# Four places of their own for the last full slot's row tiles, scaled by ScalarE, in a fused attention and mixture-of-experts kernel

## The chip, the cores and the metric

The kernel runs on one core of one Trainium2 chip. The metric is device time in microseconds (us); lower is better. The engines are named as the profile names them: PE is TensorE (PEld its weight loads), DVE is VectorE, ACT is ScalarE, POOL is GpSimd, SP is SyncE, which here only issues DMAs. L499 is line 499 of the kernel before.

## What is computed

A sigmoid attention gives 3584 tokens of 768 numbers; a gate sends each token to one of eight experts, which is two matrix products with a relu between them, and the row that comes out is scaled by two gate values.

```python
# q, k, v: (8, 12, 448, 64); x: N = 3584 tokens of D = 768; E = 8 experts, F = 1024
scores = scale * np.matmul(q, k.transpose(0, 1, 3, 2)) - np.log(S)
x = np.matmul(1.0 / (1.0 + np.exp(-scores)), v)      # then (B, H, S, D) -> (B*S, H*D)
e_idx = np.argmax(x @ w_gate, axis=1)
for e in range(E):
    mask = e_idx == e
    h = np.maximum(x[mask] @ w1[e], 0.0)
    ye = h @ w2[e]
    out[mask] = gate_w[mask, None] * eom[mask, e, None] * ye
```

## The kernel before

**Stages.** The first part of the program is the attention; it writes the rows of x to `x_dram` and, batch by batch, puts each token into the list of its expert. The second part works through *slots*: one slot is up to 448 tokens (`TB`, a full slot) or up to 240 tokens (`TM`, a partial slot) of one expert. How many slots of each kind there are is known only at run time; with this input nine run, seven full ones and then two partial ones. The last four full slots and the two partial ones stand behind branches on two counts, `full` and `part`. Where the count of full slots is used up, the program leaves that chain (the "exit") and goes to the partial slots, `half(0)`, `half(1)` and so on, each again behind a test of `part`.

**One slot.** `slot` (L542) runs layer 1 in eight steps f (L550): 18 matmuls each, three for every one of the six pieces of the depth, because each operand is split into a rounded part and a rest (`split`, L408: ACT casts, DVE subtracts). After each step ACT takes the product out of PSUM with a relu (L471) and DVE forms its rest (L472). Three PSUM places serve these products in turn (`psh`), so PE can't begin a fourth before ACT has emptied the first. In steps 1 to 4 `split_w2` splits the slot's own second weights, and behind them SP loads the first weights of the next slot (`load_w1`), which lie in the same bytes of the tile `plain` (`w1r`, `w2r`). POOL gathers the next slot's rows by an indirect DMA (L384), one or two per step. Then DVE turns these rows (`turn_x`, L429), and layer 2 follows, beside which the next slot's first weights and rows are split (`split_w1`, `split_x`, both L409 on ACT and L410 on DVE) and its second weights are loaded (`load_w2`, L395). A load into the bytes of `w1r` can only go once DVE has subtracted the weights that stood there.

**The two kinds of layer 2.** A full slot computes it in six groups of output columns (`layer2_columns`); DVE turns each back into `yq`. The sixth group is left in PSUM for the next slot, in `self.left`. A partial slot computes two row tiles t in two halves n each (`layer2`, L488): ACT scales a half into the place y (L499), and after n = 1 POOL scatters the 128 rows to `out` by an indirect DMA (L502, L537).

**What is left over.** `finish` (L504) is a generator that brings a full slot's 448 rows to `out`, in pieces between the next slot's work. Its first piece turns back the sixth group and has SP store `yq` to `y_dram` in eight DMAs (L515). The second loads two of the four row tiles back, 128 rows each and the fourth 64, into two places `ys` (L521). The third scales these two by the token weights (L526 on POOL, or L528 on ACT), scatters them, and loads the other two tiles into the same two places, which must wait until the scatters have read them. The fourth scales and scatters these. After a full slot ACT scales; behind the exit, where the weights were copied to `left_w` and `lt` is None, POOL does.

**`half(0)` in the code.** It finishes the last full slot while it computes its own rows. Its `finish` gets the places `hb` and `ys[1]`. The piece that loads tiles 0 and 1 runs at step 6 of layer 1 (L564), the piece that scales them and loads tiles 2 and 3 runs ahead of layer 2 (L578), the last piece after the first half tile (i == 0, L590). Its own two row tiles both use `ys[0]` (L582), so ACT's first write for tile 1 waits until the scatter of tile 0 has read that place. `half(1)` has nothing left to finish and uses `ys[0]` and `ys[1]`.

**Order.** The order on each engine is the program's order (`manual_schedule`); waits between engines follow from the tiles' bytes. Two scatters to `out` are taken to touch the same bytes and so wait for each other, except those that `finish` declares free of each other (L531). In `constants` and `route_tiles` four arrays of the routing, `lg`, `oh`, `turn`, `num`, are tiles of their own.

Of the kernel before, what the change touches and what calls it, by code (L numbers as in the profile page):

```python
# [8 lines left out]
F32 = mybir.dt.float32  # L9
# [3 lines left out]
AF = mybir.ActivationFunctionType  # L13
ALU = mybir.AluOpType
# [8 lines left out]
DM = H * D  # L23
DF = 1024
NT = B * S
HS = S // 2
NB = HS // 32
NCH = -(-NB // 2)
Q4 = DM // 4
G = 2  # L30
TB = 448
TM = 240
GB_, GM = TB // 32, -(-TM // 32)
# [14 lines left out]
XG = GB_ * Q4 * 4  # L48
# [3 lines left out]
def r32(ap):  # L52
    return ap.bitcast(F32)


class Kernel:
# [19 lines left out]
    def memory(self):  # L76
        self.rounded = self.pool("rounded").tile([128, ROUNDED // 4], F32R, name="rounded")
        self.plain = self.pool("plain").tile([128, PLAIN // 4], F32, name="plain")
        ps = self.pool("psum", space=PSUM).tile([128, 8, 512], F32, name="ps")
        self.ps_s = [ps[:, 0:2], ps[:, 2:4]]  # L80
        self.ps_o = [[ps[:, 4], ps[:, 5]], [ps[:, 6], ps[:, 7]]]
        self.ps_s2 = ps[:, 6:8]
        self.psh = [ps[:, i] for i in (0, 1, 2)]
        self.psy = [ps[:, i] for i in (4, 5, 3)]
        self.ps_step = [ps[:, i, 0:8] for i in (7, 3)]
        self.rot = {}
        self.beat = [None, None]
        self.hints = {2: [ET.Activation, ET.DVE, ET.Pool], 5: [ET.PE]}

        c = self.carve  # L90
        w = c(0, 3, 2, 2, DF)
        self.w1s = [[w[:, d // 2, a, d % 2] for d in range(6)] for a in range(2)]
        self.w1p = [[w[:, k, a] for k in range(3)] for a in range(2)]
        self.xs = [c(12 * DF * 4 + i * 6 * TB * 4, 6, TB) for i in range(2)]

        self.w1r = c(0, 6, DF, dt=F32)
        self.w2r = c(0, 8, DM, dt=F32)
        self.xg = c(6 * DF * 4, GB_, Q4, dt=F32)
        self.xT = c(6 * DF * 4 + XG, 6, TB, dt=F32)
        self.yq = c(6 * DF * 4 + XG, GB_, Q4, dt=F32)  # L100

    def late_memory(self):
        p = self.pool("late", reuse_waits="tile")
# [23 lines left out]
    def constants(self):  # L127
        nc = self.nc
# [8 lines left out]
            t, pattern=pattern, base=base, channel_multiplier=cm, allow_small_or_imprecise_dtypes=True)  # L137
# [18 lines left out]
        for i in range(4):  # L156
            r, at = slice(32 * i, 32 * i + 32), HS * (i % 2) + 32 * NCH * (i // 2)
# [10 lines left out]
        nc.gpsimd.memset(self.one8, 1.0)  # L168
        self.taken = cp.tile([1, E], F32, name="taken")
        nc.gpsimd.memset(self.taken, 0.0)  # L170
        self.tab_e, self.scattered = [], []
        slots = EARLY + LATE_N
        self.lts = cp.tile([128, slots, 4, 2], I32, name="lts")
        self.ltb = cp.tile([128, E, 2, 2], I32, name="ltb")
# [16 lines left out]
    def route_tiles(self):  # L191
        rp = self.pool("route")
        t = lambda n, shape, dt=F32: rp.tile(shape, dt, name=n)
        self.R = dict(
            lg=t("lg", [64, NB, 32]), oh=t("oh", [64, NB, 32]),
            turn=t("turn", [64, NB, 32]), num=t("num", [64, NB, 32]),
            mx=t("mx", [64, NB]), fi=t("fi", [64, NB]), df=t("df", [64, NB, E]), rk=t("rk", [64, NB, E]),
            sg=t("sg", [64, 3, NB, E]), posf=t("posf", [64, NB]), posi=t("posi", [128, 2, NCH], I32),
            den=t("den", [64, 2, NB]), eom=t("eom", [64, 2, NB]))
        self.nc.gpsimd.memset(self.R["oh"], 0.0)  # L200
# [225 lines left out]
    def turn_x(self, s, k):  # L426
        if s is not None:
            g, q = s["lx"].shape[1], slice(2 * k, 2 * k + 2)
            self.nc.vector.transpose(  # L429
                self.xT[:, q, 0:32 * g].rearrange("p k (g t) -> p g k t", t=32),  # L430
                self.xg[:, 0:g, 64 * k:64 * k + 64].rearrange("p g (k f) -> p g k f", f=32))

    def turn_rows(self, s, a, b):
# [10 lines left out]
    def split_x(self, s, k):  # L444
        if s is not None:
            q, n = slice(2 * k, 2 * k + 2), 32 * s["lx"].shape[1]
            self.split(self.xT[:, q, 0:n], self.xs[0][:, q, 0:n], self.xs[1][:, q, 0:n])

    def change_step(self, first):
        for _ in range(2):  # L450
# [50 lines left out]
        if n == 1:  # L501
            self.scatter(s["lt"][:, t, 0:1], y)  # L502

    def finish(self, ys):  # L504
        if self.left is None:
            return
        nc = self.nc
        ps, lt = self.left
        at = lambda t, r: self.left_at[r, t:t + 1] if lt is None else lt[r, t, 0:1]
        w = lambda t, r: self.left_w[r, t:t + 1] if lt is None else r32(lt[r, t, 1:2])  # L510
        self.turn_back(ps, 5)
        rows = self.y_dram.rearrange("(g t) (a x) -> a t g x", t=32, a=4)
        for g in (slice(0, 8), slice(8, GB_)):
            for a in range(4):
                nc.sync.dma_start(rows[a, :, g], self.yq[32 * a:32 * a + 32, g])  # L515
        yield
        sent = []
        for two in ((0, 1), (2, 3)):
            parts = [(t, slice(0, 128 if t < 3 else 64)) for t in two]
            for t, r in parts:  # L520
                nc.sync.dma_start(ys[t % 2][r], self.y_dram[128 * t:128 * t + r.stop])  # L521
            yield
            for t, r in parts:
                y = ys[t % 2][r]
                if lt is None:
                    nc.gpsimd.tensor_scalar(y, y, w(t, r), 0.0, ALU.mult, ALU.add)  # L526
                else:
                    nc.scalar.activation(y, y, AF.Copy, scale=w(t, r))  # L528
                i = self.scatter(at(t, r), y)
                for j in sent:  # L530
                    self.tc.declare_no_dep(i, j, reason="each token has one place in one list")  # L531
                sent.append(i)
            if two[0]:
                yield

    def scatter(self, at, y, parts=1):
        return self.nc.gpsimd.indirect_dma_start(  # L537
            out=self.out.rearrange("n (i e) -> (n i) e", i=parts),
            out_offset=bass.IndirectOffsetOnAxis(ap=at, axis=0),
            in_=y, in_offset=None, bounds_check=parts * NT - 1, oob_is_err=False).ins  # L540

    def slot(self, cur, nxt, side=None, begun=False, hint=None):  # L542
        nx = None
# [1 line left out]
            nx, rows, sure = nxt() if callable(nxt) else nxt  # L545
            last = -(-nx["lx"].shape[1] // 2) - 1
        n = 32 * cur["lx"].shape[1]
        fin = self.finish(self.ys if n == TB else (self.hb, self.ys[1]))
        next(fin, None)
        self.rot["y"] = 1  # L550
        for f in range(8):
# [22 lines left out]
        if n == TB:  # L574
            next(fin, None)
            self.layer2_columns(cur, nx, side, hint, fin)
            return nx
        next(fin, None)  # L578
        ws = {0: (0,), 1: (1, 2)}
        for i in range(4):  # L580
            t = i // 2
            self.layer2(cur, t, i % 2, self.ys[0 if self.left is not None else t])  # L582
            if nx is not None:
                for k in ws.get(i, ()):
                    self.split_w1(k)
                    for j in range(k, 4 if k == 2 else k + 1):
                        self.load_w2(nx, j)
                if i < 3:
                    self.split_x(nx, i)
            if i == 0:  # L590
                next(fin, None)
            if side is not None:
                next(side, None)
# [216 lines left out]
    def build(self, phases="abc"):  # L810
# [77 lines left out]
            self.left = left  # L888
        with some.Else():
            with tc.manual_schedule():  # L890
                for _ in self.finish(self.ys):
                    pass


# [33 lines left out]
```

## Time and profile before

| | us |
|---|---|
| median of 3 runs | 776.46 |
| lowest and highest run | 775.35, 779.75 |
| the profiled execution, its own time | 781.4 |
| its span, first to last instruction | 779.5 |
| PE busy | 750.4 (96%) |
| DVE, ACT, POOL busy | 414.6, 367.1, 256.5 |

The times of single instructions are from the one profiled execution; its start is 0. The attention takes about the first half of the span, the nine slots the second. PE has work in nearly all of it; in the 40 equal slices of the page the exception stands near the end, where the two partial slots run (from 683.75 us on).

### The profile page before, as it was taken

Reading aid. Unit: us, or ns where it says so; the run is one execution under the profiler, and the core shown is the slowest. Engines: PE = TensorE matmul, PEld = TensorE weight load, DVE = VectorE, ACT = ScalarE, POOL = GpSimd, SP = SyncE. Lnnn points to the kernel's source line nnn. Section 1 sums busy time; section 2 is a strip of 40 time slices with the busy share of each in tenths; the row PEclk is TensorE's granted clock in tenths of the full one; section 3 lists DMA queues with packets and bytes.
Section 4 is the critical chain, followed back from the end, with each engine's and each line's share of the span. In section 5 each row is a group of like instructions: output and inputs, shape, how many; then the busy total and the mean of one; then the engine's idle time right before and its main releaser. Section 6 shows DMA issues by size and latency. Waiting matters only on the chain. (4 is left out here: it accounts for less than half of the span.)

```text
span 779.5 us, 14531 instructions
## 1 busy us (share of the span) xinstructions
PE 750.4 (96%) x5593; PEld 557.4 (71%) x5593; DVE 414.6 (53%) x735; ACT 367.1 (47%) x433; POOL 256.5 (33%) x379
## 2 busy tenths in 40 slices
PE   9999999999999999999999999999999999998196
PEld 4344444444344489999999999999999999998196
DVE  1364646647587669444546446446446446455054
ACT  5666666666776544043335235235235234243044
POOL 5002202021343354265342342342342342334341
PEclk9999999999999999999999999999999999999588
DMA  8465665757787454665764764764755764774611
GB/s 301 141 172 149 187 165 155 201 134 212 233 280 217 110 159 146 168 170 178 244 190 173 263 170 175 263 170 175 263 169 176 264 168 176 257 219 158 242 47 39
DMA packets 90647, 145.77 MB, mean 187 GB/s; under 512 B 16751, under 2 KB 67311, under 8 KB 90560
## 3 DMA queue, kind: packets, MB, share of 16 engines
q1 hardware_dynamic: 79808, 119.22, 50.7%
q0 software_dynamic: 9680, 24.53, 9.2%
q10 hardware_dynamic: 1072, 0.92, 0.5%
q8 instruction: 47, 0.77, 0.4%
q14 instruction: 40, 0.33, 0.1%
HBM read 118.40 MB, written 32.72 MB: 194 GB/s over the span
## 5 line engine op out<-in xcount | busy, mean ns | idle before, releaser
L664 ACT ACTIVATE a<-ps,bias_s 128x896 f32<-128x896 f32 x168 | 168.7, 1007 | 87.2 <-PE ps L662 84.9
L459 PE MATMUL ps<-rounded 128*128 128x448 f32 (+1 forms) x432 | 151.5, 351 | 20.7 <-ACT rounded L409 19.7
L662 PE MATMUL ps<-q,k 64*64 64x448 f32 x1344 | 158.2, 543 | 0.8 <-ACT a L664 0.5
L384 POOL DMA_INDIRECT plain<-x_dram,lxs x112 | 111.2, 993 | 143.3 <-ACT h L471 61.8
L671 PE MATMUL ps<-a,v 64*64 64x448 f32 x1344 | 156.0, 536 | 0.0
L460 PE MATMUL ps<-rounded 128*128 128x448 f32 (+1 forms) x432 | 150.7, 349 | 0.2 <-DVE rounded L410 0.2
L461 PE MATMUL ps<-rounded 128*128 128x448 f32 (+1 forms) x432 | 150.5, 348 | 0.0
L471 ACT ACTIVATE h<-ps 128x448 fp32r<-128x448 f32 (+1 forms) x72 | 36.4, 506 | 217.8 <-PE ps L461 217.3
L481 PE MATMUL ps<-h,w2l 128*128 128x448 f32 x336 | 122.9, 366 | 0.0
L480 PE MATMUL ps<-h,w2h 128*128 128x448 f32 x336 | 122.8, 366 | 0.0
L482 PE MATMUL ps<-h,w2h 128*128 128x448 f32 x336 | 122.8, 366 | 0.0
L410 DVE TENSOR_TENSOR rounded<-plain,rounded 128x2048 fp32r<-128x2048 f32 (+5 forms) x63 | 96.5, 1567 | 30.7 <-ACT rounded L409 30.7
L662 PEld LDWEIGHTS ps<-q,k 64*64 64x64 f32 x1344 | 50.3, 134 | 77.5 <-issue 70.7
L671 PEld LDWEIGHTS ps<-a,v 64*64 64x64 f32 x1344 | 50.9, 133 | 75.5 <-issue 72.6
L472 DVE SCALAR_TENSOR_TENSOR h<-ps,h 128x448 fp32r<-128x448 f32 (+1 forms) x72 | 41.3, 574 | 118.3 <-ACT h L471 107.9
L459 PEld LDWEIGHTS ps<-rounded 128*128 128x128 f32 x432 | 82.6, 191 | 27.0 <-ACT rounded L409 19.9
L409 ACT CAST rounded<-plain 128x2048 fp32r<-128x2048 f32 (+5 forms) x63 | 81.9, 1334 | 18.0 <-DVE plain L429 16.7
L460 PEld LDWEIGHTS ps<-rounded 128*128 128x128 f32 x432 | 82.6, 191 | 5.5 <-DVE rounded L410 0.4
L461 PEld LDWEIGHTS ps<-rounded 128*128 128x128 f32 x432 | 82.6, 191 | 5.2
L537 POOL DMA_INDIRECT out<-y,lts x24 | 42.8, 1783 | 105.5 <-ACT y L528 102.6
L486 DVE STREAM_TRANSPOSE plain<-ps 128x448 f32<-128x448 f32 x42 | 27.1, 645 | 80.5 <-PE ps L482 74.4
L410 DVE TENSOR_TENSOR w2l<-plain,w2h 128x768 fp32r<-128x768 f32 x72 | 65.8, 954 | 3.5 <-ACT w2h L409 1.0
(146 smaller groups left out, 708.4 us busy)
## 6 DMA issues: line engine op xcount, KB each, us to landing
plain<-w SPq DMA_DIRECT2D x40, 768.0 KB
plain<-w SPq DMA_DIRECT2D x27, 1024.0 KB
k<-kT SPq DMA_DIRECT2D x23, 448.0 KB
q<-qT SPq DMA_DIRECT2D x23, 448.0 KB
x_dram<-xt SPq DMA_DIRECT2D x30, 336.0 KB
v<-vm SPq DMA_DIRECT2D x23, 384.0 KB
y<-y_dram SPq DMA_DIRECT2D x19, 384.0 KB
y_dram<-plain SPq DMA_DIRECT2D x28, 192.0 KB
```

The source lines that it names most:

```text
L384: self.paced(self.nc.gpsimd.indirect_dma_start(out=self.xg[:, g], out_offset=None, in_=x4, in_offset=bass.IndirectOffsetOnAxis(ap=s["lx"][ ...
L409: self.nc.scalar.copy(hi, raw)
L410: self.nc.vector.tensor_tensor(lo, raw, r32(hi), ALU.subtract)
L459: nc.tensor.matmul(ps, wh[d][:, c], xh[:, d, 0:n], start=(d == 0), stop=False)
L460: nc.tensor.matmul(ps, wh[d][:, c], xl[:, d, 0:n], start=False, stop=False)
L461: mm = nc.tensor.matmul(ps, wl[d][:, c], xh[:, d, 0:n], start=False, stop=(d == 5))
L480: nc.tensor.matmul(ps, wh, hh[:, f], start=(f == 0), stop=False)
L481: nc.tensor.matmul(ps, wl, hh[:, f], start=False, stop=False)
L482: nc.tensor.matmul(ps, wh, hl[:, f], start=False, stop=(f == 7))
L662: qk = nc.tensor.matmul(ps[half[h], j, 0:S], k[half[j], e, o:o + 64], q[half[j], e], start=True, stop=True)
L664: self.beat[0] = nc.scalar.activation(at[u % 3], ps[:, :, 0:S], AF.Sigmoid, bias=self.bias_s, scale=1.0 / math.sqrt(D)).ins
L671: nc.tensor.matmul(self.ps_o[e][h][half[j], 0:S], v[half[h], e, c, j], a[half[h], j], start=(i in ((0, 3 if h else 4)[e],)), stop=(i == (2 ...
```

## The change

Behind the exit the four row tiles of the last full slot get four places: two stretches of `plain` that a partial slot leaves free (`spare`: behind the eight gathered groups in the bytes of `xg`, and behind the shorter turned rows `xTm` in the bytes of `yq`), `hb`, and the front of a new tile `rbuf`, which holds the four routing arrays. All four loads are issued in one piece at step 6 of layer 1. The pieces that scale and scatter run after the first and after the second half tile of layer 2 (i < 2); the piece ahead of layer 2 is gone. ACT scales in every case; POOL's scaling is dropped. The slot's own two tiles use `ys[0]` and `ys[1]`. All scatters to `out`, of `finish` and of `layer2`, are declared free of each other. A partial slot's rows are turned into `xTm`, which is 256 columns wide, in place of the first 256 columns of `xT`. After a full slot the order of loads, scalings and scatters stays.

```diff
+        self.xTm = c(6 * DF * 4 + XG, 6, 32 * GM, dt=F32)
+        self.spare = c(6 * DF * 4 + GM * Q4 * 4, DM, dt=F32), c(6 * DF * 4 + XG + 6 * 32 * GM * 4, DM, dt=F32)
...
+        self.rbuf = t("rbuf", [64, 4 * NB * 32])
         self.R = dict(
-            lg=t("lg", [64, NB, 32]), oh=t("oh", [64, NB, 32]),
-            turn=t("turn", [64, NB, 32]), num=t("num", [64, NB, 32]),
+            **{n: self.rbuf[:, NB * 32 * i:NB * 32 * i + NB * 32].rearrange("p (c x) -> p c x", c=NB)
+               for i, n in enumerate(("lg", "turn", "num", "oh"))},
...
-    def finish(self, ys):
+    def finish(self, n):
...
+        ys = self.ys * 2 if n == TB else (*self.spare, self.hb, self.rbuf[:, 0:DM])
+        parts = [(t, slice(0, 128 if t < 3 else 64)) for t in range(4)]
...
+        def load(two):
+            for t, r in two:
+                nc.sync.dma_start(ys[t][r], self.y_dram[128 * t:128 * t + r.stop])
+
         yield
-        sent = []
-        for two in ((0, 1), (2, 3)):
-            parts = [(t, slice(0, 128 if t < 3 else 64)) for t in two]
-            for t, r in parts:
-                nc.sync.dma_start(ys[t % 2][r], self.y_dram[128 * t:128 * t + r.stop])
+        load(parts[0:2] if n == TB else parts)
+        yield
+        for two in (parts[0:2], parts[2:4]):
+            for t, r in two:
+                nc.scalar.activation(ys[t][r], ys[t][r], AF.Copy, scale=w(t, r))
+                self.scatter(at(t, r), ys[t][r])
+            if n == TB and two[0][0] == 0:
+                load(parts[2:4])
             yield
-            for t, r in parts:
-                y = ys[t % 2][r]
-                if lt is None:
-                    nc.gpsimd.tensor_scalar(y, y, w(t, r), 0.0, ALU.mult, ALU.add)
-                else:
-                    nc.scalar.activation(y, y, AF.Copy, scale=w(t, r))
-                i = self.scatter(at(t, r), y)
-                for j in sent:
-                    self.tc.declare_no_dep(i, j, reason="each token has one place in one list")
-                sent.append(i)
-            if two[0]:
-                yield
...
+        for j in self.sent:
+            self.tc.declare_no_dep(i, j, reason="each token has one place in one list")
+        self.sent.append(i)
...
-        fin = self.finish(self.ys if n == TB else (self.hb, self.ys[1]))
+        fin = self.finish(n)
...
-        next(fin, None)
         ws = {0: (0,), 1: (1, 2)}
...
-            self.layer2(cur, t, i % 2, self.ys[0 if self.left is not None else t])
+            self.layer2(cur, t, i % 2, self.ys[t])
...
-            if i == 0:
+            if i < 2:
                 next(fin, None)
```

## Rows read from the trace of the kernel before

**Rows 1.** The page's 40 slices: PE's busy share and granted clock, in tenths.

```profile
PE   9999999999999999999999999999999999998196
PEclk9999999999999999999999999999999999999588
```

**Rows 2.** PE's timeline: start, duration, line, operation, idle time before and releaser.

```profile
683.75 0.35 PE L459 MATMUL ps<-rounded 128*128 128x240 f32 x1 [0.97 <-DVEq L870]
...
717.86 0.27 PE L461 MATMUL ps<-rounded 128*128 128x240 f32 x1
...
737.84 0.57 PE L459 MATMUL ps<-rounded 128*128 128x240 f32 x1 [19.70 <-ACT rounded L409]
```

**Rows 3.** Stretches: length, each engine's busy time (instructions), granted clock, DMA share, GB/s.

```profile
683.75:699.95 16.20, 16.20 (x144) 16.20 (x145) 10.20 (x16) 8.49 (x15) 7.26 (x8) 1.00 0.75 210
...
716.63:756.21 39.58, 19.72 (x145) 19.25 (x145) 10.32 (x16) 9.99 (x18) 16.82 (x16) 0.70 0.45 155
...
737.84:744.67 6.83, 6.67 (x30) 6.39 (x30) 1.48 (x3) 1.61 (x4) 2.95 (x3) 0.50 0.22 75
...
756.21:773.00 16.79, 16.79 (x98) 16.49 (x96) 10.90 (x10) 8.96 (x10) 1.54 (x2) 1.00 0.08 31
```

**Rows 4.** ACT's timeline in the first partial slot's layer 2.

```profile
704.48 0.58 ACT L499 ACTIVATE y<-ps,ltb 128x384 f32<-128x384 f32 x1 [3.90 <-PE ps L498]
704.96 2.41 ACT L409 CAST rounded<-plain 128x2048 fp32r<-128x2048 f32 x2
708.51 0.58 ACT L499 ACTIVATE y<-ps,ltb 128x384 f32<-128x384 f32 x1 [1.14 <-PE ps L498]
708.99 4.23 ACT L409 CAST rounded<-plain 128x2048 fp32r<-128x2048 f32 x3
736.70 0.58 ACT L499 ACTIVATE y<-ps,ltb 128x384 f32<-128x384 f32 x1 [23.48 <-DMA out<-y,ltb]
```

**Rows 5.** POOL's timeline there.

```profile
707.90 3.42 POOL L526 TENSOR_SCALAR hb<-hb,leftw 128x768 f32<-128x768 f32 x1 [7.58 <-DVE plain L429]
711.61 2.78 POOL L537 DMA_INDIRECT out<-hb,leftat  x1 [0.28 <-POOL hb L526]
...
717.25 1.01 POOL L537 DMA_INDIRECT out<-y,leftat  x1 [0.28 <-POOL y L526]
...
726.71 0.93 POOL L537 DMA_INDIRECT out<-y,leftat  x1 [0.28 <-POOL y L526]
733.53 1.00 POOL L537 DMA_INDIRECT out<-y,ltb  x1 [5.89 <-DMA out<-y,leftat]
```

**Rows 6.** SP's timeline, the times at which it issues DMAs.

```profile
697.84 0.68 SPq L521 DMA_DIRECT2D hb<-y_dram  x1
...
717.74 0.32 SPq L521 DMA_DIRECT2D hb<-y_dram  x1
...
723.26 0.41 SPq L395 DMA_DIRECT2D plain<-w  x1
```

**Rows 7.** Stretches as in rows 3, cut where the DMA traffic changes.

```profile
692.00:698.00 6.00, 6.00 (x56) 6.00 (x55) 5.64 (x9) 4.03 (x7) 2.79 (x4) 1.00 0.95 253
698.00:706.00 8.00, 8.00 (x54) 8.00 (x54) 0.85 (x3) 2.27 (x4) 1.25 (x2) 1.00 1.00 384
706.00:708.00 2.00, 2.00 (x14) 2.00 (x13) 2.00 (x4) 1.37 (x2) 0.10 (x1) 1.00 0.39 153
...
724.00:734.00 10.00, 0.00 (x0) 0.00 (x0) 0.00 (x0) 0.00 (x0) 2.29 (x3) 0.50 1.00 384
```

**Rows 8.** DVE's timeline beside that layer 2.

```profile
705.96 1.90 DVE L429 STREAM_TRANSPOSE plain<-plain 128x512 f32<-128x512 f32 x3 [4.94 <-DMA plain<-w]
707.78 2.85 DVE L410 TENSOR_TENSOR rounded<-plain,rounded 128x2048 fp32r<-128x2048 f32 x2
710.93 5.34 DVE L410 TENSOR_TENSOR rounded<-plain,rounded 128x2048 fp32r<-128x2048 f32 x3 [0.30 <-ACT rounded L409]
```

**Rows 9.** ACT's groups of instructions, one shape each, from 600 to 680 us.

```profile
L528 ACT ACTIVATE y<-y,lts 128x768 f32<-128x768 f32 x6 | 5.4, 930 | 13.6 <-DMA y<-y_dram 13.6
```

More of the change, by code (lines that the diff above doesn't have):

```diff
@@ L170, in constants @@
         nc.gpsimd.memset(self.taken, 0.0)
-        self.tab_e, self.scattered = [], []
+        self.tab_e, self.scattered, self.sent = [], [], []
         slots = EARLY + LATE_N
@@ L429, in turn_x @@
             self.nc.vector.transpose(
-                self.xT[:, q, 0:32 * g].rearrange("p k (g t) -> p g k t", t=32),
+                (self.xT if g == GB_ else self.xTm)[:, q].rearrange("p k (g t) -> p g k t", t=32),
                 self.xg[:, 0:g, 64 * k:64 * k + 64].rearrange("p g (k f) -> p g k f", f=32))
@@ L446, in split_x @@
             q, n = slice(2 * k, 2 * k + 2), 32 * s["lx"].shape[1]
-            self.split(self.xT[:, q, 0:n], self.xs[0][:, q, 0:n], self.xs[1][:, q, 0:n])
+            self.split((self.xT if n == TB else self.xTm)[:, q], self.xs[0][:, q, 0:n], self.xs[1][:, q, 0:n])
     def change_step(self, first):
@@ L515, in finish, with scatter @@
                 nc.sync.dma_start(rows[a, :, g], self.yq[32 * a:32 * a + 32, g])
+        def load(two):
+            for t, r in two:
+                nc.sync.dma_start(ys[t][r], self.y_dram[128 * t:128 * t + r.stop])
         yield
-        sent = []
-        for two in ((0, 1), (2, 3)):
-            parts = [(t, slice(0, 128 if t < 3 else 64)) for t in two]
-            for t, r in parts:
-                nc.sync.dma_start(ys[t % 2][r], self.y_dram[128 * t:128 * t + r.stop])
-            yield
-            for t, r in parts:
-                y = ys[t % 2][r]
-                if lt is None:
-                    nc.gpsimd.tensor_scalar(y, y, w(t, r), 0.0, ALU.mult, ALU.add)
-                else:
-                    nc.scalar.activation(y, y, AF.Copy, scale=w(t, r))
-                i = self.scatter(at(t, r), y)
-                for j in sent:
-                    self.tc.declare_no_dep(i, j, reason="each token has one place in one list")
-                sent.append(i)
-            if two[0]:
-                yield
-    def scatter(self, at, y, parts=1):
-        return self.nc.gpsimd.indirect_dma_start(
-            out=self.out.rearrange("n (i e) -> (n i) e", i=parts),
+        load(parts[0:2] if n == TB else parts)
[6 more added lines that the diff above has]
+                load(parts[2:4])
+            yield
+    def scatter(self, at, y):
+        i = self.nc.gpsimd.indirect_dma_start(
+            out=self.out,
             out_offset=bass.IndirectOffsetOnAxis(ap=at, axis=0),
-            in_=y, in_offset=None, bounds_check=parts * NT - 1, oob_is_err=False).ins
+            in_=y, in_offset=None, bounds_check=NT - 1, oob_is_err=False).ins
+        for j in self.sent:
+            self.tc.declare_no_dep(i, j, reason="each token has one place in one list")
+        self.sent.append(i)
     def slot(self, cur, nxt, side=None, begun=False, hint=None):
@@ L890, in build @@
             with tc.manual_schedule():
-                for _ in self.finish(self.ys):
+                for _ in self.finish(TB):
                     pass
```

## The prediction, made before the changed kernel was built

> **What bounds the kernel now.** I read the page's slices first. PE is busy in tenths of nine in every slice but the last four, where it goes 8, 1, 9, 6, and its granted clock falls to 5 in the slice after the hole [rows 1]. So PE is the bound for 720 us, the hole of nearly a slice of 19.5 us is the one place with something to win, and a change there is worth what it does to the hole. PE's timeline gives its edges: after the matmul at 717.86, the twelfth of the second partial slot's first step, PE stands 19.70 us until a cast of ACT's, L409 [rows 2]. The clock is the second item: it was granted in full before the hole, is 0.50 from 737.84 to 744.67, when PE is at work again, and then full [rows 3], that is 1.2 GHz and then 2.4 GHz. The two partial slots do the same layer 1, 144 matmuls. The first takes 16.20 us, the second 39.58 us [rows 3]; the difference, 23.38 us, is what hole and clock cost together. Split: the hole is 717.86 to 737.84 less one step of 0.11 (16.20/144), 19.87 us; the rest, 3.5 us, is the slow clock.
>
> Whom PE waits for is read backwards. ACT stands in its own queue before the write of its first half tile of tile 1 (L499 at 736.70), 23.48 us, released by the DMA `out<-y,ltb` [rows 4]. The cast PE needs, the last third of the next rows, stands right behind it. That DMA is the scatter of tile 0 out of `ys[0]`; POOL issues it only at 733.53, after 5.89 us of waiting for the scatter at 726.71 to finish [rows 5], and before that POOL went through four scalings and four scatters in its queue, of which the third and fourth had to wait for loads into the places of the first and second. SP's timeline shows these loads: tile 0 at 697.84, but tile 2 only at 717.74, when the first scatter had let go of `hb`, and the second weights behind it at 723.26 [rows 6]. So it is one chain: two places for four tiles, a scatter at its end, ACT behind the scatter, PE behind ACT.
>
> **The change, part by part.**
> *Own tiles keep their places.* Tile 1 goes to `ys[1]`, which `finish` no longer uses in a partial slot. ACT's wait of 23.48 us has no cause left: the place was last read by the previous slot's scatters, over 20 us earlier. Removed: the hole, 19.87, and the clock that follows it, 3.5.
>
> *Four places, four loads at step 6.* SP issues at 697.84 what it issued before [rows 6] and two loads more, with no wait on a scatter. What is late next is their landing. Traffic runs at 384 GB/s until 706 and at 153 in the next two us [rows 7], so the first weights of the next slot and the two loads are through at about 707.5. Tiles 2 and 3 are 192 rows of 3072 bytes, 0.59 MB, at 384 GB/s 1.5 us more: about 709. In order of issue tile 0 lands by about 707, tile 1 by 708, tiles 2 and 3 by 709.
>
> The rows gathered for the next slot compete with this traffic. DVE begins to turn them at 705.96 [rows 8]; I can't tell from the trace whether two more loads make that later, so I bound it by 0 and 1.5 us and take 0.5, since the gathers were issued before the loads.
>
> By the Trainium skill, "DMA: Bandwidth & Descriptors", Two DMAs through the same engine are not ordered, descriptors of one queue at least start in order, so all four loads would queue behind the last first-weight load however early they are issued, and the gathers, in another queue, would share the engines. By that the sum would have the 1.5 us in full for the landing of tile 3 and less for tile 0; this is how the rows on the traffic read, too, and no row shows one load by itself.
>
> *ACT scales.* Four operations of 0.93 us [rows 9], pairs overlapping to some 1.75, 3.5 us in all, go onto ACT's queue inside layer 2, which ends with the casts PE waits for. ACT's order becomes: write 704.48, casts to 707.37 [rows 4], scale tiles 0 and 1, write, three casts, scale tiles 2 and 3, write, cast of the last third. With T the time at which the first scaling can start, the last third is cast at T + 1.75 + 0.5 + 4.2 + 1.75 + 0.5 + 0.6 = T + 9.3. T is 707.4 if ACT is not held, 708 with the landing above; I take 708, so 717.3, and DVE's rest, 0.7 us more, 718.0. DVE on its own path gets there at about the same time: the second third of `w1` is cast at T + 4.15 = 712.2, then two rests of weights of 2.25 each and two short ones of 0.7 [rows 8] make 718.1. PE asks for the cast at 716.63 + 12 x 0.112 = 717.97 and for the rest 0.11 later. So the stall that takes the place of the hole is between 0 and, with T and DVE both 1.5 late, 1.6 us. I take 0.5, from the end to which T = 708 is nearer. A wait of 0.97 us, at 683.75, left the clock at 1.00 [rows 2, 3], so I add nothing for the clock.
>
> *POOL* loses four scalings (the first took 3.42 us [rows 5]) and the waits between scatters. It issues six scatters from about 710 on, each 1.0 us alone and 2.78 beside DVE's splits [rows 5], which end at about 718: by 722 in all, 725 at worst. Behind them in its queue are the eight gathers of the second partial slot; they are paced by PE's steps to 733, and nothing but the turning of rows that no slot uses waits for them. Cost nothing, and if that cover went, ACT has about 4 us free in the last layer 2 (9 us busy of 16.79 [rows 3]).
>
> By the Trainium skill, "SBUF — State Buffer", Two separate sides, DVE and GpSimd share one pair of ports and the one that comes second is blocked for a whole instruction; Who interferes with whom there infers that DVE's subtractions spare the writing of DMA descriptors. The 2.78 us beside such subtractions against 1.01 at 717.25 speaks against that inference. By the page's inference the scatters would be through at 717, by the row at 722 to 725, and the time is the same by either.
>
> *Second weights.* SP's queue now has nothing but these behind the four loads. Each can go when DVE has freed its bytes: the first at about 710.5, the second at 714.5, the third and fourth at 717. Four of them are 3.1 MB, 8.2 us at 384 GB/s [rows 7]; with scatters of 2.2 MB beside them, the last is there at about 724. They are asked for from step 1 to step 4 of the second slot, the first at about 721.1, the last at 727. So no cost, with 3 us to spare; the rival below takes the cover away.
>
> *The rest.* One tile for the routing arrays: DVE alone writes three of them and PE is busy all through the attention [rows 1]; its cost lies between nothing and DVE waits that PE's queue hides; I take 0. The freed scatters after full slots: in those slots POOL waits for ACT's scalings and not for scatters, 0. The narrower `xTm` has the same number of elements, 0. The tail is the same last scatter.
>
> **Sum.** 23.4 - 0.5 = 22.9 us. Of the profiled execution's 781.4 that is 758.5. That execution is 4.9 us above the median of the runs, whose 776.46 the prediction is compared with; the hole is a chain of DMAs and waits that is there in any run, so I take the same 22.9 off the median: 753.6.
>
> **The rivals.**
> *The second weights come late.* Speaking for it: the traffic beside gathers ran at 253 GB/s from 692 to 698 [rows 7]. At that rate 5.3 MB from 710.5 on take 21 us, to 731.5, and ACT stands at the fourth split instead of emptying PSUM, 4.5 us late; layer 2 needs the parts only in its course. Against: the 384 of 724 to 734, when four such loads and scatters ran together. If it happens PE loses 2 to 5 us, perhaps with a slow clock of 3.5 behind it: 756 to 762, middle 758.
> *The wait stays.* Some dependence that I don't see, as between the stretches of `plain`, keeps ACT behind the scatter, or SP behind it: then the hole remains, 776.5. Against: the places are disjoint bytes, and the code already cuts `plain` that way.
> *Slower: ACT held at the scaling.* Before, POOL stood and waited for loads while ACT went on to cast the weights; now everything ACT does for the next slot is queued behind the load of tile 0. If T is late, PE resumes at T + 9.3 + 0.7. With the slow clock in both cases the change breaks even at T = 728 and is slower by over 0.5% (3.9 us) from T = 732. A load that waits for as long as tile 2 did (to 717.74 plus about 3 us) gives T = 721, still faster, 769; if the four loads came behind the second weights, whose traffic ends at 734 [rows 7], T = 735 and the time 776.5 + 7 = 783.5. Against: in SP's order they stand ahead of these.
>
> **How the numbers follow.** Forecast 753.6, chance 0.80; late weights 0.11; the wait stays 0.05; slower 0.04. The forecast's own range is 23.4 to 21.8 off the median, 753.1 to 754.7, widened by how the three runs lie about theirs (-1.1, +3.3): 752 to 758. The late weights reach to 762; up to 760.5 leaves out about half of them, and the other two cases. At the low end the two executions' difference of 4.9 may hold some of the hole's size; 751. About 0.5% is what a measurement of this kernel can tell from no change. Faster by more than that: forecast and late weights, 0.91; within it 0.05; slower 0.04.
>
> **What would show it.** In the changed kernel's profile the slice with 1 should be gone and the granted clock full to the end; the second partial slot's layer 1 should take 16 to 18 us, not 39.6; the wait on `out<-y,ltb` should not be on ACT; ACT's four scalings should stand between 707 and 717 with waits under 2 us; the second weights should be issued between 710 and 718. I am wrong if PE still has a hole over 3 us in that slot, if the first split of its second weights waits for a DMA, or if the scalings wait past 710.

## The result and the profile after

The changed kernel takes 757.44 us (median of 4 runs, 756.03 to 758.83); the kernel before, run beside it, 775.9 us (774.75 to 779.75). The ratio is 0.9754, with a 95% interval of 0.9714 to 0.9793: 18.5 us less. On another chip the two gave 757.07 and 777.16 us, ratio 0.9753 (0.9723 to 0.9782), 20.1 us less. The profiled execution of the changed kernel took 758.83 us, its span is 757.0.

The page's slices of the changed kernel, which answer to [rows 1]:

```profile
PE   9999999999999999999999999999999999999996
PEclk9999999999999999999999999999999999999999
```

The hole is gone and the clock is full to the end. The stretches of the two partial slots (columns as in [rows 3]) are layer 1 of the first, layer 1 of the second, layer 2 of the second:

```profile
684.37:700.50 16.13, 16.13 (x144) 16.13 (x145) 10.20 (x16) 8.50 (x15) 7.24 (x8) 1.00 0.75 236
717.19:733.32 16.13, 16.13 (x146) 16.13 (x145) 10.30 (x17) 8.85 (x17) 12.17 (x11) 1.00 0.70 266
733.32:750.20 16.88, 16.81 (x98) 16.49 (x96) 10.90 (x10) 8.96 (x10) 1.66 (x2) 1.00 0.10 35
```

Both layers 1 take 16.13 us; the second took 39.58 before. PE never waits in between. ACT's timeline shows the new order, where [rows 4] ended with a wait of 23.48 us:

```profile
705.04 0.58 ACT L502 ACTIVATE y<-ps,ltb 128x384 f32<-128x384 f32 x1 [3.88 <-PE ps L501]
705.52 1.90 ACT L412 CAST rounded<-plain 128x2048 fp32r<-128x2048 f32 x1
707.68 0.62 ACT L412 CAST rounded<-plain 128x512 fp32r<-128x512 f32 x1 [0.27 <-DVE plain L432]
708.21 1.76 ACT L531 ACTIVATE plain<-plain,leftw 128x768 f32<-128x768 f32 x2
709.87 0.56 ACT L502 ACTIVATE y<-ps,ltb 128x384 f32<-128x384 f32 x1
710.34 4.23 ACT L412 CAST rounded<-plain 128x2048 fp32r<-128x2048 f32 x3
714.46 0.94 ACT L531 ACTIVATE hb<-hb,leftw 128x768 f32<-128x768 f32 x1
715.30 0.92 ACT L531 ACTIVATE rbuf<-rbuf,leftw 64x768 f32<-64x768 f32 x1
716.13 0.56 ACT L502 ACTIVATE y<-ps,ltb 128x384 f32<-128x384 f32 x1
716.59 0.61 ACT L412 CAST rounded<-plain 128x512 fp32r<-128x512 f32 x1
...
728.38 1.57 ACT L412 CAST w2h<-plain 128x768 fp32r<-128x768 f32 x2 [0.20 <-DMA plain<-w]
```

The four scalings stand at 708.21 to 716.2, none waits for a load, and the last third of the next rows is cast by 717.20, before PE asks for it. The last line is the fourth split of the second weights: it waits 0.20 us for the weights, so these were just in time. SP's timeline, to be read beside [rows 6], shows when they were issued; its last line holds the third and the fourth, the fourth at 717.5:

```profile
698.65 1.55 SPq L524 DMA_DIRECT2D plain<-y_dram  x2
700.26 0.42 SPq L524 DMA_DIRECT2D hb<-y_dram  x1
700.72 0.48 SPq L524 DMA_DIRECT2D rbuf<-y_dram  x1
...
711.03 0.41 SPq L398 DMA_DIRECT2D plain<-w  x1
...
714.59 0.39 SPq L398 DMA_DIRECT2D plain<-w  x1
...
716.79 2.40 SPq L398 DMA_DIRECT2D plain<-w  x2
```

All four loads go at step 6, with no wait on a scatter, and the first second weights at 711.03 in place of 723.26.

### The profile page after: what moved, and what is told of

It reads as the page before. It is cut to its first block, busy times and chain, and to the rows that moved or that the text cites. A ratio compares the mean times of both kernels' runs of the same rounds, so it can differ in the third digit from the quotient of the medians.

```text
span 757.0 us, 14551 instructions
## 1 busy us (share of the span) xinstructions
PE 746.7 (99%) x5593; PEld 555.6 (73%) x5593; DVE 414.2 (55%) x735; ACT 370.0 (49%) x437; POOL 249.9 (33%) x375
## 5 line engine op out<-in xcount | busy, mean ns | idle before, releaser
L462 PE MATMUL ps<-rounded 128*128 128x448 f32 (+1 forms) x432 | 149.9, 347 | 1.4 <-DVEq L873 1.4
L464 PE MATMUL ps<-rounded 128*128 128x448 f32 (+1 forms) x432 | 149.2, 345 | 0.0
L463 PE MATMUL ps<-rounded 128*128 128x448 f32 (+1 forms) x432 | 149.1, 345 | 0.0
L462 PEld LDWEIGHTS ps<-rounded 128*128 128x128 f32 x432 | 81.2, 188 | 7.5 <-issue 2.4
L464 PEld LDWEIGHTS ps<-rounded 128*128 128x128 f32 x432 | 81.3, 188 | 5.2
L463 PEld LDWEIGHTS ps<-rounded 128*128 128x128 f32 x432 | 81.3, 188 | 5.1
```

The source lines that it names most:

```text
L462: nc.tensor.matmul(ps, wh[d][:, c], xh[:, d, 0:n], start=(d == 0), stop=False)
L463: nc.tensor.matmul(ps, wh[d][:, c], xl[:, d, 0:n], start=False, stop=False)
L464: mm = nc.tensor.matmul(ps, wl[d][:, c], xh[:, d, 0:n], start=False, stop=(d == 5))
```

## The experiments

The kernels below ran on three chips, each beside the kernel before, whose median was 777.2, 777.4 and 777.8 us there. The kernel before against itself gave a ratio of 1.0003, with an interval of 0.9986 to 1.0020, so a difference of 1 us between two kernels is not told from noise.

**Which execution of the kernel before is the usual one?** The sum had been made against an execution of 781.4 us, 4.9 above the median. Two more executions of the kernel before were profiled.

> The kernel before once more. Theory 1 (the hole in the second partial slot is not the same length in every execution, and the profiled one of before had a long one): the median stays at 776 and a new profile below 781 has a sum of hole and slow clock (layer 1 of that slot less 16.2 us) that is smaller than 23.4 by about as much as its own time lies below 781.4. Theory 2 (the executions differ elsewhere): 23.4 again, and the first partial slot starts at another time than 683.75 us.

> The kernel before a third time, for one more profile. If the hole is what varies, layer 1 of the second partial slot is between 35 and 40 us and rises with the execution's own time (36.0 us at 776.9, 39.6 at 781.4); if not, it is 36 or 39.6 whatever the time.

Medians 777.46 (12 runs, 776.0 to 781.0) and 778.13 (8 runs, 775.7 to 781.3). The profiled executions took 776.94 and 781.29. Layer 1 of the second partial slot in the first of them, then in the second:

```profile
715.69:751.70 36.01, 18.50 (x145) 18.03 (x145) 10.91 (x18) 10.00 (x18) 17.00 (x15) 0.76 0.45 160
```

```profile
716.71:755.98 39.27, 19.72 (x146) 19.25 (x146) 10.32 (x16) 10.00 (x18) 16.75 (x16) 0.70 0.45 157
```

So 36.0 at 776.9, 39.3 at 781.3, 39.6 at 781.4, as theory 1 had it. Of the 4.4 us between the spans of the shortest and the longest of the three (775.1 and 779.5), 3.6 lie in this stretch and 0.9 ahead of the partial slots, which begin at 682.83 in place of 683.75. POOL's timeline of the shorter execution, beside [rows 5], shows the first place at which they part:

```profile
707.01 0.91 POOL L526 TENSOR_SCALAR hb<-hb,leftw 128x768 f32<-128x768 f32 x1 [7.60 <-DMA hb<-y_dram]
708.21 2.78 POOL L537 DMA_INDIRECT out<-hb,leftat  x1 [0.28 <-POOL hb L526]
```

Here POOL's first scaling starts at 707.01, takes 0.91 us, and the scatter goes at 708.21. DVE's subtractions begin 0.23 us behind it in this execution:

```profile
707.24 9.14 DVE L410 TENSOR_TENSOR rounded<-plain,rounded 128x2048 fp32r<-128x2048 f32 x5
```

In the long executions (781.3 and 781.4 us) the scaling starts at 707.90 and 708.76, when DVE's subtractions already run (from 707.78 [rows 8] and 707.76), takes 3.42 and 2.55 us, and the scatter goes at 711.6. SP loads tile 2 at 713.10 in the short one, at 717.74 and 717.88 in the long ones. A scaling that is 0.23 us ahead of the subtractions, and not 0.12 us behind them, lets the first scatter go 3.4 us earlier (0.9 of them because the partial slots begin earlier), and the chain with it. This is read from three executions; no run here fixes the order of the two engines. By the Trainium skill, "SBUF — State Buffer", Who interferes with whom, a DVE instruction with two inputs in SBUF contends with a GpSimd instruction that reads SBUF, and the one that issues first holds the ports for its whole length; the trace agrees, 0.91 us ahead of the subtractions and 2.5 to 3.4 beside them.

**One part alone: own places.** The kernel before with a place of its own for tile 1.

```diff
+        self.spare = c(6 * DF * 4 + GM * Q4 * 4, DM, dt=F32)
...
-        fin = self.finish(self.ys if n == TB else (self.hb, self.ys[1]))
+        fin = self.finish(self.ys if n == TB else (self.hb, self.spare))
...
-            self.layer2(cur, t, i % 2, self.ys[0 if self.left is not None else t])
+            self.layer2(cur, t, i % 2, self.ys[t])
```

> The kernel before, in which only the partial slot's own tiles keep their places: finish uses hb and one free stretch of plain, layer 2 writes ys[0] and ys[1]. Still two places for four tiles, POOL scaling and scatters that wait for each other. My theory (two chains, one behind the other): ACT's wait of 23.5 us is gone, and with it the hole at 717.9; but SP still issues tile 2's load at about 717.7 and the second weights at 723, so the first split of these, asked for at 721, stands until about 727 and PE loses 4 to 8 us: 764 (760 to 768). Rival (the shared place was all of it): 757, like the whole change. Rival (the scatters hold everything): 776.

765.8 us (764.3 to 766.2), ratio 0.9852 (0.9827 to 0.9876). The time is as expected, but by luck: two stretches make it, and I had named only the smaller. ACT's timeline:

```profile
724.30 1.57 ACT L410 CAST w2h<-plain 128x768 fp32r<-128x768 f32 x2 [3.50 <-DMA plain<-w]
...
748.20 0.62 ACT L410 CAST rounded<-plain 128x512 fp32r<-128x512 f32 x1 [7.26 <-DVE plain L430]
```

The wait of 23.5 us is gone. The split of the second weights waits 3.50 us, but PE runs ahead of it, and layer 1 takes 17.99 us, 1.9 more than undisturbed. The other line is in the last layer 2: ACT waits 7.26 us for rows turned for a slot that doesn't run, and the last scaling of the kernel stands behind that. Counted from the start of that layer 2, this scaling comes 3.3 us later than in the changed kernel, and from it to the end of the span another 1.4 us more pass.

**One part alone: free scatters.** The kernel before with every scatter to `out` declared free of all others.

```diff
-                i = self.scatter(at(t, r), y)
-                for j in sent:
-                    self.tc.declare_no_dep(i, j, reason="each token has one place in one list")
-                sent.append(i)
+                self.scatter(at(t, r), y)
...
+        for j in self.sent:
+            self.tc.declare_no_dep(i, j, reason="each token has one place in one list")
+        self.sent.append(i)
```

> The kernel before with nothing but the scatters to out all free of each other. My theory: the wait of 5.9 us ahead of the scatter of tile 0 goes, so this is issued at about 728 in place of 733.5 and ACT goes on about 5.5 us earlier; the second weights land at about 734 and are asked for from some 735 on, so they don't take it back: 770.5 (768 to 773). Rival (POOL was late for loads, not for scatters): 776.

775.3 us (12 runs, 773.6 to 776.7) beside 777.16, ratio 0.9979 (0.9961 to 0.9997): by the ratio 1.6 us, where 5.5 were expected: my 770.5 fell, and the rival's 776 is nearer, though not for its reason. POOL's line, then ACT's, then the traffic between them:

```profile
725.16 1.00 POOL L534 DMA_INDIRECT out<-y,ltb  x1 [0.30 <-issue]
```

```profile
732.41 0.58 ACT L499 ACTIVATE y<-ps,ltb 128x384 f32<-128x384 f32 x1 [19.39 <-DMA out<-y,ltb]
```

```profile
725.00:732.00 7.00, 0.00 (x0) 0.00 (x0) 0.00 (x0) 0.00 (x0) 1.00 (x1) 0.50 0.97 356
```

The scatter did go without the wait, but it lets go of `ys[0]` only 7.3 us after its start, against 3.2 in [rows 4, 5], where the second weights were through. The kernel before at that place:

```profile
734.00:736.70 2.70, 0.00 (x0) 0.00 (x0) 0.00 (x0) 0.00 (x1) 0.53 (x1) 0.50 0.40 158
```

So the scatter is slow where the second weights run beside it, at 356 in place of 158 GB/s; that they are the reason is argued here, and tested below in another kernel. In the short execution of the kernel before, whose first scaling took 0.91 us as it did here, the scatter is issued at 730.31 and ACT writes at 733.47; here it is 725.16 and 732.41. Of the 5.2 us that the scatter is earlier, 1.1 are left to ACT. What the wait cost, the traffic took.

**Both parts.** Own places and free scatters, the two diffs above together; still two places for four tiles.

> The kernel before with two parts of the change, own places for the slot's own tiles and all scatters free of each other; still two places for the four tiles, POOL scaling, tile 2 loaded behind the first scatter and the second weights behind it. My theory, after the traces of own_only and of the changed kernel with the waits back: in own_only the first split of the second weights stood 3.5 us and layer 1 lost 1.9 us, and the rest, some 6 us, came from POOL, whose waits make the gathers late; with the scatters free only the first stays: 759.5 (758 to 761). Rival (the late weights are the larger part, as I said ahead of own_only): 763 to 765.

761.4 us (758.95 to 765.7), ratio 0.9785 (0.9754 to 0.9815): over the expected 759.5 (758 to 761) and under the rival's 763. Against own places alone the freed scatters gave 4.4 us, where some 6 were expected. The profiled execution is the longest of the six, 765.7. Its ACT and its layer 1 of the second partial slot:

```profile
729.20 1.56 ACT L410 CAST w2h<-plain 128x768 fp32r<-128x768 f32 x2 [7.21 <-DMA plain<-w]
```

```profile
717.33:740.49 23.16, 18.47 (x146) 18.27 (x146) 9.19 (x14) 8.68 (x16) 15.15 (x15) 0.85 0.75 261
```

The last scaling isn't held any more. In this execution POOL's first scaling met DVE's subtractions (2.66 us), tile 2 was loaded at 718.27, and the second weights were issued 6.1 us after the slot's start, against 3.0 in the profile of the kernel with own places alone. Layer 1 takes 7.0 us more than undisturbed. So the two places for four tiles cost 1.9 us where the first scaling was early (own places alone) and 7.0 where it was late, one execution of each; at the median it is 4.3, 761.4 against 757.1.

**One part undone: own places.** The changed kernel with both own tiles in `ys[0]`.

```diff
-            self.layer2(cur, t, i % 2, self.ys[t])
+            self.layer2(cur, t, i % 2, self.ys[0 if self.left is not None else t])
```

> The changed kernel with one part undone: the slot's own two tiles share ys[0] again. My theory (the place was only harmful because its scatter was issued at the end of a chain of loads and scatters): tile 0's scatter is issued at about 713.5 and has read ys[0] by 717, so ACT's write for tile 1 moves from 716.1 to about 717 and the last third of the rows is cast 1 us later: 758.5 (757 to 760). Rival (the shared place itself costs the hole): over 765.

764.9 us (760.6 to 766.5), ratio 0.9826 (0.9795 to 0.9858): my 758.5 fell, and the rival's "over 765" is just missed by the median: three of the six runs lie above it, two at 760.6 and 760.7. I had the scatter read its place within 4 us. ACT's line and the traffic:

```profile
721.13 0.58 ACT L502 ACTIVATE y<-ps,ltb 128x384 f32<-128x384 f32 x1 [5.66 <-DMA out<-y,ltb]
```

```profile
713.00:721.00 8.00, 5.29 (x35) 5.09 (x33) 3.61 (x3) 2.48 (x4) 4.48 (x3) 1.00 0.99 380
```

POOL began that scatter at 712.76; it let go at 721.13, 8.4 us later, with the DMA engines busy for 0.99 of the time. Whether the weights are to blame or the scatters themselves was asked next, with the first partial slot's loads of the next second weights left out.

```diff
-                        self.load_w2(nx, j)
+                        if self.left is None:
+                            self.load_w2(nx, j)
```

> The changed kernel with the shared place ys[0] (764.9 us), in which the first partial slot doesn't load the second weights of the next: that part of the result is computed from what stands in the place. My theory (the scatter out of ys[0] is slow because 3.1 MB of weights are on the same DMA engines): the scatter issued at about 712.8 has read its place by about 717 in place of 721.1, ACT goes on at 716 to 717.5 and PE has a hole of at most 1 us: 757 to 759. Rival (a scatter takes 6 to 8 us in any traffic, from its own issue and the scatters beside it): 763 to 766.

759.3 us (757.8 to 760.1), ratio 0.9754 (0.9731 to 0.9777). ACT's line and the traffic there:

```profile
717.22 0.58 ACT L502 ACTIVATE y<-ps,ltb 128x384 f32<-128x384 f32 x1 [2.12 <-PE ps L464]
```

```profile
713.00:717.20 4.20, 4.20 (x30) 4.20 (x29) 3.24 (x3) 2.10 (x3) 3.59 (x3) 1.00 0.44 171
```

The profile says that this write waited 2.12 us for L464, a matmul of layer 1, of which it needs nothing; I take it for the scatter out of the same place. Begun at 712.39, that had let go by 717.22, after 4.8 us at most. So 5.6 us of the 7.8 that the shared place costs at the median are the weights' traffic. Whether the rest, 2.2, is real is open: the ratio to the kernel before is 0.9754, that of the changed kernel 0.9753, while layer 1 of this profile takes 17.81 us, 1.7 more than undisturbed.

**One part undone: free scatters.** The changed kernel in which only the four of `finish` are free of each other.

```diff
+        sent = []
         for two in (parts[0:2], parts[2:4]):
...
-                self.scatter(at(t, r), ys[t][r])
+                self.scatter(at(t, r), ys[t][r], sent)
...
-    def scatter(self, at, y):
+    def scatter(self, at, y, sent=None):
...
-        for j in self.sent:
+        sent = [] if sent is None else sent
+        for j in sent:
             self.tc.declare_no_dep(i, j, reason="each token has one place in one list")
-        self.sent.append(i)
+        sent.append(i)
```

> The changed kernel in which scatters wait for each other again, except the four of finish among themselves. My theory (only POOL feels it): three scatters get a wait of some 3 us each, POOL's gathers come up to 8 us later, which the last layer 2 covers by 4: 757.4 to 760. Rival (the freed scatters are what let ACT go on): over 765.

762.2 us (759.65 to 762.9), ratio 0.9816 (0.9788 to 0.9845): 5.1 over the changed kernel, more than expected, though ACT isn't held where the rival had it. Layer 1 of the second partial slot is at 16.13 us, as in the changed kernel. The loss is in POOL's queue and comes out at the end. POOL's timeline, then ACT's:

```profile
717.81 0.98 POOL L539 DMA_INDIRECT out<-y,ltb  x1 [5.63 <-ACT y L502]
725.30 1.14 POOL L539 DMA_INDIRECT out<-hb,leftat  x1 [6.51 <-ACT h L474]
...
732.83 0.98 POOL L539 DMA_INDIRECT out<-y,ltb  x1 [4.41 <-DMA out<-rbuf,leftat]
734.12 0.99 POOL L387 DMA_INDIRECT plain<-x_dram,lxb  x1 [0.30 <-issue]
...
742.97 0.95 POOL L387 DMA_INDIRECT plain<-x_dram,lxb  x1 [0.30 <-remote]
```

```profile
746.91 0.62 ACT L412 CAST rounded<-plain 128x512 fp32r<-128x512 f32 x1 [7.69 <-DVE plain L432]
...
753.00 0.59 ACT L502 ACTIVATE y<-ps,ltb 128x384 f32<-128x384 f32 x1
```

Three scatters wait 5.6, 6.5 and 4.4 us. The profile puts the first two waits down to instructions of ACT that these scatters don't need; I take them, too, for the scatters before them, which are slow in the weights' traffic. The eight gathers behind start at 734.12 in place of 720.43, the last at 742.97 in place of 732.86; ACT waits 7.69 us for rows of a slot that doesn't run, and its last scaling is at 753.00, where the changed kernel has it at 750.23 (counted from the start of layer 1, 3.7 us later). The last scatter behind it takes 2.11 us in place of 1.00, beside DVE's subtractions for that slot. If that is the path, leaving out the preparation of that slot must give the time back although the scatters wait:

```diff
-        half = lambda k: self.slot(lists(k), mid(k + 1) if k + 1 < E else None)
+        half = lambda k: self.slot(lists(k), mid(k + 1) if k + 1 < 2 else None)
```

> The changed kernel with the waits between scatters back (762.2 us), in which the second partial slot prepares no slot behind it: its gathers, turned rows, splits and loads, all for a slot that doesn't run with this input, are left out. My theory (late gathers hold ACT's last scalings): 757, the time of the changed kernel, although the scatters wait as before. Rival (the waiting scatters themselves, or their traffic, cost the 5 us): 761 to 763.

757.97 us (five runs from 756.6 to 758.2, one at 764.0, which I can't explain), ratio 0.9751 (0.9718 to 0.9784): 4.3 of the 5.1 us came back. The waits between the scatters are still there, and here the profile puts the first of them down to the scatter before it:

```profile
718.31 0.98 POOL L539 DMA_INDIRECT out<-y,ltb  x1 [6.00 <-DMA out<-plain,leftat]
```

So the cost is the preparation of a slot that doesn't run, which late gathers make late. The changed kernel without that preparation was not run; in its profile ACT's last scaling, at 750.23, waits 2.63 us for PE, so it is not held by the preparation there.

**One part undone: the scaling engine.** POOL scales behind the exit, all else as changed.

```diff
-                nc.scalar.activation(ys[t][r], ys[t][r], AF.Copy, scale=w(t, r))
+                if lt is None:
+                    nc.gpsimd.tensor_scalar(ys[t][r], ys[t][r], w(t, r), 0.0, ALU.mult, ALU.add)
+                else:
+                    nc.scalar.activation(ys[t][r], ys[t][r], AF.Copy, scale=w(t, r))
```

> The changed kernel with POOL scaling the four tiles again behind the exit, everything else as changed. My theory (the engine that scales doesn't matter once nobody waits for the scatters): ACT is 3.5 us freer, POOL's scatters come out up to 10 us later, PE still has no hole: 757.4, within 1.5. Rival (POOL's lateness matters): the gathers of the second partial slot are behind the scatters, the rows turned for the slot that doesn't run come late, and ACT and DVE hold the last scaling of the kernel: 759 to 763.

757.35 us (756.2 to 757.8), beside 757.07 for the changed kernel in the same comparison: no difference that this can tell. POOL's last gather starts at 734.22 in place of 732.86, and nothing that is needed waits for it. The changed kernel itself, run beside it:

> The changed kernel once more, for the comparison with its variants on one chip: 757.4 by both theories. Its profile should again show no hole: layer 1 of both partial slots at 16.1 us, the clock full.

757.07 us (756.2 to 757.5). Its profile has layer 1 of the second partial slot at 16.67 us, 0.5 more than undisturbed. ACT's first scaling stands 0.89 us there for its load, DVE 1.74 us for the cast behind it, and PE waits 0.27 us for DVE once; ACT waits 0.71 us for the last of the second weights.

**The price of an ACT that is held.** The changed kernel with the loads of tiles 2 and 3 behind the second weights.

```diff
-        load(parts[0:2] if n == TB else parts)
+        load(parts[0:2])
...
             yield
+            if n < TB and two[0][0] == 0:
+                load(parts[2:4])
```

> The changed kernel with the loads of tiles 2 and 3 behind the second weights in SP's queue, at the piece in which ACT scales them. It prices the rival in which ACT is held at a scaling: ACT stands there until the loads have landed, behind 3.1 MB of weights whose last part is issued at 717.5 and is through at about 724 to 726, so ACT goes on at about 727, the cast of the last third comes 3 us later, and PE has a hole of some 11 to 13 us with a slow clock of up to 3.5 us behind it: 770 (766 to 775). Rival (ACT isn't on the path, PE waits for weights alone): 757 to 759.

772.6 us (770.1 to 773.1), ratio 0.9939 (0.9916 to 0.9962), as the theory had it. ACT stands at the third scaling:

```profile
724.65 0.93 ACT L531 ACTIVATE hb<-hb,leftw 128x768 f32<-128x768 f32 x1 [11.52 <-DMA hb<-y_dram]
```

PE has a hole from 716.54 to 727.44, 10.9 us, with a clock at half until 732:

```profile
727.44 0.57 PE L462 MATMUL ps<-rounded 128*128 128x240 f32 x1 [10.62 <-ACT rounded L412]
```

Where the two loads stand in SP's queue is worth some 15 us, most of the gain.

## Why the prediction was right, point by point

**The sum held for the execution it was made against.** 781.4 less 22.9 was to be 758.5; the profiled execution of the changed kernel took 758.83. The chain was read rightly: with the place and the loads changed, ACT's wait, PE's hole and the slow clock went together, and layer 1 fell from 39.58 to 16.13 us. That is 23.45 us; the partial slots began 0.6 us later and what follows layer 1 took 0.4 us more.

**The step that failed is the one from that execution to the median**, "the hole is a chain of DMAs and waits that is there in any run, so I take the same 22.9 off the median". The hole is there in any run, but it is not of one length: 39.6, 39.3 and 36.0 us of layer 1 in three executions of the kernel before, rising with their time. An execution of 776.9 us has a hole and a clock that cost 36.0 - 16.1 = 19.9 us, not 23.4; taken off 776.9 that gives 757.0, which is what the changed kernel takes. So the forecast of 753.6 was too low by 3.8, the measured 757.44 lies inside its own range of 752 to 758, and the clue was in the table: the profiled execution lay 4.9 above the median, and above all three runs. The prediction did allow that the excess might lie in the hole, but at the wrong end: if it does, the hole of a usual execution is shorter, the gain smaller and the time higher, up to 758.5, while 751 was set down for it. That the range held is in part luck: its upper end of 758 came from how the three runs lie about their median, and not from the hole. Where such an excess lies should be asked of the stretch that the change takes away.

**The four places and the loads.** The turn of the rows was to come 0.5 us later and T to be 708.0; measured from the first L502, which is 0.56 us later than before, they are 706.37 (0.4 later) and 707.65. In the second profile of the changed kernel, measured in the same way, T is 708.56, because tile 0's load held the first scaling for 0.89 us. The stall in PE was to be 0.5, between 0 and 1.6; it was 0 in one execution and some 0.5 in another.

**ACT's scaling.** Four operations of 0.93 us as costed, and no cost, as costed. But none was saved by it either: with POOL scaling the time is the same. In the kernel before, by the reading of its three executions, POOL's scaling decides when tile 2 can be loaded; the kernel before with ACT scaling was not run.

**POOL, "cost nothing".** The sum was right, the account behind it wasn't complete. I gave the freed scatters no value; undone, they cost 5.1 us. POOL's gathers are paced by PE only if POOL is there in time, and what I set down as nothing but the turning of rows that no slot uses stands in ACT's queue ahead of the kernel's last scalings. The 4 us of cover that I named were used up: with the waits back the last scaling came 3.7 us later and the last scatter took 1.1 us more.

**Second weights, "3 us to spare".** The mis-sized term: I had the last of them there at 724 and asked for at 727. The DMA engines were busy until 727, with scatters and gathers beside the weights:

```profile
713.00:727.00 14.00, 14.00 (x114) 14.00 (x113) 9.42 (x11) 9.64 (x16) 10.65 (x9) 1.00 0.99 385
```

The fourth split waited 0.20 us for them at 728.38 (0.71 in another execution). The cover was nearly nothing, not 3 us; the rival of late weights was closer than its 0.11 said.

**The rest, put at 0.** The first partial slot starts at 684.37 and 682.69 us in the two profiles of the changed kernel, and between 682.83 and 683.85 in the three of the kernel before: no cost or gain is seen ahead of it.

**The rivals.** That the wait stays did not happen. The held ACT was built and costs some 15 us with two of the loads behind the weights (all four behind them, the case of 783.5, was not built): the rule T + 9.3 was for the first scaling; for the third, from which four short steps remain, 724.65 gives the resumption at 727.44, 2.8 us later, and the slow clock behind it. The kernel stays faster than before, as this rival's break-even point had it. What I had no rival for is how long a scatter takes in the weights' traffic, and with that how much the shared place costs even when its scatter goes early: 7.8 us at the median.

The parts don't add up: own places alone give some 12 us, free scatters alone 1.6, and the two together 16; the four places with their early loads give the last 4.3. ACT's scaling has no part in these 4.3: with POOL scaling and the four places the time is 757.35.

## What to carry to other kernels

Price a removed wait from more than one execution if the profiled one lies off the median, and look for what sets its length, as here the order of two engines. An operation whose result nobody uses still counts if an engine's queue has needed work behind it: work that prepares the next turn after the last turn is such a case. And a place that a DMA must let go of is only as free as the other traffic at that time lets it be.

## What the runs showed of the hardware

- A scatter of 128 rows let go of its place 3.2 us after its start at 158 GB/s [rows 4, 5], after 4.8 us at most at 171 GB/s, and after 7.3 and 8.4 us beside the second weights at 356 and 380 GB/s. POOL took 1.0 us over the first and the third of these, 1.9 us over the other two.
- The same scaling on POOL took 0.91 us when it began ahead of DVE's subtractions and 2.55 to 3.42 us beside them.
- After PE had stood for 4.0 us (with the shared place), 10.6 us (late loads), 17.4 us (the short execution of the kernel before) and 19.7 us [rows 2], the granted clock was at half for 3.4, 4.7, 4.1 and 6.8 us once it worked again: a longer wait did not always mean a longer time at half. In the first of these the clock was still full when PE began again, and fell 1.2 us later.
- Not settled: the six runs with the shared place fall into two groups, 760.6 to 760.7 and 764.7 to 766.5 us, and only one of the second was profiled.
